# A streaming attention kernel: ScalarE's pairs in one branch loop, four VectorE steps merged or moved

## The chip, the cores and the metric

The kernel runs on one core of one Trainium2 chip. The metric is the device time of that core in microseconds (us); lower is better. Engines are named as in the profile: PE is TensorE's matmuls, PEld its weight loads, DVE is VectorE, ACT is ScalarE, POOL is GpSimd, SP is the engine that issues most DMAs. The suffix q (ACTq, SPq) means the engine's sequencer.

## The reference, cut to what matters

One token (512 values) attends to a cache of 32 heads x 16384 positions x 128, and a small gated MLP of the same token is mixed in:

```python
# shapes: x (1,1,512); k_cache, v_cache (1,32,16384,128) bf16; wq (512,4096); wo (4096,512)
g = sigmoid((x * gate_w).sum(-1, keepdims=True))
q = (x @ wq) split in 32 heads
p = softmax(q k^T / sqrt(128)); o = p v
a = o @ wo
b = gmlp(x, w_in, w_sp, b_sp, w_out)      # small
return g * a + (1 - g) * b
```

K and V are 134 MB each. Every byte is read once and used for one query, so the kernel is a stream from HBM with arithmetic beside it.

## The kernel before

Heads are taken in 16 pairs. One pair has one K load and one V load of 8.39 MB each; three buffers of that size take turns. Load n may be issued when the user of load n-3 is done. SP issues them:

```python
k_at = [max(2 * i - 1, 0) for i in range(NP)]            # K0 K1 V0 K2 V1 K3 V2 ...
v_at = [min(2 * i + 2, 2 * NP - 1) for i in range(NP)]
...
wait = [user[n - 3]] if n >= 3 else ...                  # exps(i) frees a K buffer, values(i) a V buffer
sp.op(lambda e: e.dma_start(out=buf[n % 3][:, ...], in_=src[:, ...]), wait=wait, ...)
```

So the load of V1 waits for the exps of pair 1, V2 for those of pair 2 and so on; K loads from K3 on wait for PE's values. For each pair DVE multiplies K by q in four quarters and PE and DVE sum them to scores, ACT takes the exponentials (`exps`), PE multiplies by V, and ACT copies the result out of the PSUM bank and zeroes it (`renew`):

```python
def exps(e, i):
    take(e, red_s)                      # the scores of pair i are there
    ...                                 # two activations Exp, 64 rows each
def renew(e):
    drain(e).then_inc(zer_s, 1)         # copy the value bank out
    take(e, zer_s)
    e.copy(out=d_ps, in_=zero[:, :]).then_inc(drn_s, 1)

def act_pairs(e):
    e.wait_ge(*p_zero)
    exps(e, 0)
    exps(e, 1)
    with e.Fori(2, NP) as i:
        renew(e)
        exps(e, i)
    renew(e)
    ...
```

The set-up before the pairs (queries, gate, gMLP) and the tail after them (scale, transpose, product with wo) are straight-line code on all engines. The output projection's weights wo are the last bytes of the stream.

The softmax here doesn't subtract the row's maximum and nothing guards it: scores larger than these inputs give would overflow.

## Time and profile before

The time was 652.02 us (median of 3 runs, 651.7 to 652.5).

| | before |
|---|---|
| span of the profiled run | 650.2 us |
| bytes read | 279.6 MB, 430 GB/s over the span |
| DMA engines | 9 tenths or more in all slices but the last |
| busy PE / DVE / ACT | 65% / 52% / 7% |

From the page of the kernel before: the span, the busy times, the DMA row (busy tenths in 40 slices) and the rate in each slice.

```profile
span 650.2 us, 7753 instructions
...
PE 424.3 (65%) x2474; PEld 47.0 (7%) x1312; DVE 335.8 (52%) x159; ACT 45.8 (7%) x112; POOL 2.2 (0%) x10
...
DMA  9999999999999999999999999999999999999998
GB/s 384 463 419 452 452 395 443 452 443 395 452 452 395 443 452 448 391 452 452 403 435 452 448 391 452 452 431 407 452 452 395 443 452 439 399 435 468 392 428 342
...
```

No engine is busy for even 70% of the span, but the DMA engines always are. The Trainium skill ("DMA: Bandwidth & Descriptors", "Where 436 GB/s comes from") gives a ceiling of 435.2 GB/s. This trace agrees: successive 8.39 MB loads land 19.35 us apart (26 loads between the landings at 76.8 and 579.9 us), which is 433.5 GB/s. The same section also says that for loads from HBM a core's share of about 358 GB/s binds; this core, running alone, is above that.

From the chain of waits that ended last, before (start, duration, what):

```profile
...
617.70 0.33 SPq L643
...
619.02 28.88 DMA bufs<-in_A_wo_dram
...
647.94 0.65 PE ps_all L716 x8
...
648.61 0.41 DVE res L731
```

The span ends with the last pieces of wo, then eight matmuls and one copy. SP issues wo's loads at 617.70, when ACT's last exps have freed their buffer (the link before, cut here).

From the timeline of SP, before: the K and V loads as they are issued (start, duration, what).

```profile
...
65.79 0.33 SPq L638 DMA_DIRECT2D bufs<-in_A_k_cache_dram  x1
90.87 0.33 SPq L638 DMA_DIRECT2D bufs<-in_A_v_cache_dram  x1
...
122.68 0.33 SPq L638 DMA_DIRECT2D bufs<-in_A_v_cache_dram  x1
...
```

The profile also tells when each load landed: the K2 load issued at 65.79 took 30.4 us, so it landed at 96.2. ("Landed" means that the last piece of the load had arrived.) The V1 load was issued at 90.87, when the queue still had 96.2 - 90.87 = 5.3 us of work. I call this number the *queue left* at issue. For the steady pairs it is 11 to 12 us for V loads and 21 to 22 us for K loads.

From the timeline before, around the first exps of ACT; the last bracket is the idle time before the piece:

```profile
...
63.14 0.69 DVE L564 TENSOR_REDUCE s_sb<-ps_all 128x64 f32<-128x512 f32 x1 [3.93 <-DVEq L86]
63.96 1.28 ACT L592 ACT_TABLE_LOAD   x1 [29.56 <-ACTq L86]
...
65.79 0.33 SPq L638 DMA_DIRECT2D bufs<-in_A_k_cache_dram  x1
...
```

The Exp table is loaded between the end of the scores (63.83) and the first exps; K2's load follows at 65.79.

From the timeline before, the set-up steps in question:

```profile
...
1.18 0.27 DVE L278 MEMSET sel<- 32x258 uint32 x1 [1.18 <-PEq L762]
...
2.20 3.04 DVE L301 MEMSET ps_all<- 128x3584 f32 x1 [0.74 <-issue]
...
12.03 0.41 DVE L314 TENSOR_TENSOR xg_row<-x_row,gw_row 1x512 bf16<-1x512 bf16 x1 [5.33 <-DMA wb_row<-in_B_b_sp_dram]
...
14.17 0.16 DVE L327 COPY wbf<-ps_all 128x2 f32<-128x2 f32 x1 [0.94 <-ACT gm_sb L325]
...
17.13 0.55 PE L345 MATMUL ps_all<-bufs,xb 128*128 x1 [3.27 <-DMA bufs<-in_B_w_in_dram]
```

VectorE writes `sel` at 1.18, waits until 12.03 for a small DMA, copies `wbf` at 14.17, and PE then waits until 17.13 for w_in. From the same timeline, the tail:

```profile
...
629.44 0.24 DVE L667 TENSOR_SCALAR rl<-rl,g_sb 128x32 f32<-128x32 f32 x1
...
641.17 0.19 DVE L669 TENSOR_TENSOR o_sb<-ps_all,rl 128x32 bf16<-128x32 f32 x1 [11.49 <-PE ps_all L531]
...
647.94 0.38 PEld L716 LDWEIGHTS ps_all<-bufs,o 128*1 128x1 bf16 x8 [0.40 <-DMA bufs<-in_A_wo_dram]
...
```

The scale step (L667) runs at 629.44, long before the multiply (L669) at 641.17. PE's last eight matmuls wait 0.40 us for wo.

### The profile page before, as it was taken

Reading aid. Unit: us, or ns where it says so; the run is one execution under the profiler, and the core shown is the slowest. Engines: PE = TensorE matmul, PEld = TensorE weight load, DVE = VectorE, ACT = ScalarE, POOL = GpSimd, SP = SyncE. Lnnn points to the kernel's source line nnn. Section 1 sums busy time; section 2 is a strip of 40 time slices with the busy share of each in tenths; the row PEclk is TensorE's granted clock in tenths of the full one; section 3 lists DMA queues with packets and bytes.
Section 4 is the critical chain, followed back from the end, with each engine's and each line's share of the span. In section 5 each row is a group of like instructions: output and inputs, shape, how many; then the busy total and the mean of one; then the engine's idle time right before and its main releaser. Section 6 shows DMA issues by size and latency. Waiting matters only on the chain. (4 is left out here: it accounts for less than half of the span.)

```text
span 650.2 us, 7753 instructions
## 1 busy us (share of the span) xinstructions
PE 424.3 (65%) x2474; PEld 47.0 (7%) x1312; DVE 335.8 (52%) x159; ACT 45.8 (7%) x112; POOL 2.2 (0%) x10
## 2 busy tenths in 40 slices
PE   0646687847477574857757486584748857478678
PEld 0000000000101000010000101000010100001022
DVE  3457839256380835628165370835628174465600
ACT  2210000100001000010100001000000100001011
POOL 1000000000000000000000000000000000000000
PEclk9959798958889796888969679796977969698979
DMA  9999999999999999999999999999999999999998
GB/s 384 463 419 452 452 395 443 452 443 395 452 452 395 443 452 448 391 452 452 403 435 452 448 391 452 452 431 407 452 452 395 443 452 439 399 435 468 392 428 342
DMA packets 6203, 279.60 MB, mean 430 GB/s; under 512 B 695, under 2 KB 826, under 8 KB 1210
## 3 DMA queue, kind: packets, MB, share of 16 engines
q1 hardware_dynamic: 6194, 279.58, 99.6%
q8 instruction: 1, 0.02, 0.0%
q10 hardware_dynamic: 8, 0.00, 0.0%
HBM read 279.58 MB, written 0.00 MB: 430 GB/s over the span
## 5 line engine op out<-in xcount | busy, mean ns | idle before, releaser
L579 DVE TENSOR_TENSOR bufs<-bufs,qb x64 | 281.4, 4418 | 170.8 <-DVEq L86 170.8
L91 PE MATMUL ps_all<-bufs,ident 128*128 x960 | 258.8, 423 | 0.0
L496 PE MATMUL ps_all<-bufs,ident 128*128 x64 | 28.6, 446 | 154.2 <-PEq L86 153.9
L106 PE MATMUL ps_all<-bufs,p_t 128*8 x1024 | 82.5, 396 | 30.1 <-PEq L86 20.1
L564 DVE TENSOR_REDUCE s_sb<-ps_all 128x64 f32<-128x512 f32 x64 | 44.0, 687 | 93.1 <-DVEq L86 93.1
L91 PE MATMUL ps_all<-zero,ident 128*8 128x512 bf16 (+2 forms) x167 | 59.5, 388 | 0.0
L592 ACT ACTIVATE p_t<-s_sb 64x256 f32 (+1 forms) x32 | 13.3, 415 | 433.1 <-ACTq L86 432.7
L496 PEld LDWEIGHTS ps_all<-bufs,ident 128*128 128x128 bf16 x64 | 6.3, 99 | 365.6 <-issue 365.6
L106 PEld LDWEIGHTS ps_all<-bufs,p_t 128*8 x1024 | 19.4, 83 | 163.1 <-issue 161.6
L531 PE MATMUL ps_all<-pick,d_sb 128*128 128x2 f32 x128 | 17.0, 255 | 16.5 <-PEq L86 16.5
L531 PEld LDWEIGHTS ps_all<-pick,d_sb 128*128 128x128 f32 x128 | 15.7, 193 | 34.7 <-issue 34.7
L601 ACT COPY d_sb<-ps_all 128x512 f32<-128x512 f32 x16 | 9.4, 586 | 105.4 <-ACTq L86 105.4
L606 ACT CAST ps_all<-zero 128x512 f32<-128x512 bf16 x15 | 8.8, 589 | 1.7
L666 DVE RECIPROCAL rl<-ps_all 128x32 f32<-128x32 f32 x1 | 0.4, 357 | 12.2 <-PE ps_all L552 12.2
L381 DVE TENSOR_TENSOR bufs<-ps_all,ident 128x896 f32<-128x896 f32 x2 | 2.1, 1086 | 8.6 <-PE ps_all L91 8.6
L669 DVE TENSOR_TENSOR o_sb<-ps_all,rl 128x32 bf16<-128x32 f32 x1 | 0.2, 191 | 11.5 <-PE ps_all L531 11.5
L592 ACT ACTIVATION_READ_ACCUMULATOR p_t<-s_sb (+1 forms) x32 | 5.9, 185 | 0.0
L321 PE MATMUL ps_all<-xgw,const-float32-1.0 1*128 1x3 f32 x2 | 0.6, 360 | 8.0 <-DVE xgw L317 8.0
L91 PE MATMUL ps_all<-bufs,xb 128*128 x12 | 5.0, 552 | 0.0
L106 PE MATMUL ps_all<-bufs,u 128*1 x14 | 2.6, 372 | 3.1 <-ACT ps_all L427 2.4
L345 PE MATMUL ps_all<-bufs,xb 128*128 x4 | 2.3, 574 | 3.3 <-DMA bufs<-in_B_w_in_dram 3.3
L106 PE MATMUL ps_all<-bufs,xb 128*64 x32 | 3.6, 380 | 0.0
(76 smaller groups left out, 40.2 us busy)
## 6 DMA issues: line engine op xcount, KB each, us to landing
bufs<-in_A_k_cache_dram SPq DMA_DIRECT2D x2, 4096.0 KB, 36.2
bufs<-in_A_v_cache_dram SPq DMA_DIRECT2D x1, 5120.0 KB, 34.5
bufs<-in_A_wq_dram SPq DMA_DIRECT2D x1, 4096.0 KB, 12.3
bufs<-in_A_v_cache_dram SPq DMA_DIRECT2D x1, 2048.0 KB, 39.0
bufs<-in_A_wo_dram SPq DMA_DIRECT2D x1, 2048.0 KB, 25.4
bufs<-in_B_w_in_dram SPq DMA_DIRECT2D x1, 1792.0 KB, 15.5
bufs<-in_A_v_cache_dram SPq DMA_DIRECT2D x1, 1024.0 KB, 41.0
bufs<-in_A_wo_dram SPq DMA_DIRECT2D x1, 1024.0 KB, 27.6
```

What stands on the lines that cost most here:

```text
L91: ins = eng.matmul(out, lhsT=lhsT, rhs=rhs, **flags).ins
L106: ins = eng.matmul(bank[0:m, 0:n], lhsT=lhsT, rhs=rhs, **flags).ins
L321: g_ok = pe.op(lambda e: e.matmul(g_ps, lhsT=ones_f[0:1, :], rhs=xgw[:, :], start=True, stop=True), wait=[xgw_ok], mark=True)
L345: if n else matmul_on(nc, e, lambda: e.matmul(args[0], lhsT=args[1], rhs=args[2], **flags), [at, (xa, 0)]))
L381: dve.op(lambda e, h=h, zh=zh: e.tensor_tensor(out=zm[:, 2 * h * ZB:2 * (h + 1) * ZB].rearrange("p (b m k) -> p b m k", b=2, k=FhC), in0=z ...
L496: matmul_on(nc, e, lambda: e.matmul(s3, lhsT=ident[:, :], rhs=k3[:, :, 0:W], start=True, **flags), [(kw, 0)])
L531: ins = e.matmul(o2, lhsT=d_sb[:, r * Dh:(r + 1) * Dh], rhs=pick[:, r * 2:(r + 1) * 2], start=False, stop=False, skip_group_check=True)
L564: return e.tensor_reduce(out=s_sb[:, c * QK:(c + 1) * QK], in_=s_ps[c % 2].rearrange("p (j w) -> p j w", w=W), axis=AX.X, op=ALU.add)
L579: e.tensor_tensor(out=k3, in0=k3, in1=qi, op=ALU.mult).then_inc(mul_s, 1)
L592: e.activation(out=p_t[rows, bass.ds(at, NG * 8)].rearrange("p (t c) -> p t c", c=8)[:, :, 4 * s:4 * s + 4], in_=s_sb[rows, :].rearrange(" ...
L601: return e.copy(out=d_sb[:, :], in_=d_ps)
L606: e.copy(out=d_ps, in_=zero[:, :]).then_inc(drn_s, 1)
```

## The change

The intent: ScalarE's instructions become one loop without peeled copies, its Exp table is loaded early, and VectorE loses three instructions and one wait. Main parts of the diff (line shifts and unchanged context cut):

```diff
-    for t in [L_sb, p_t, zero]:
+    for t in [sel, L_sb, p_t, zero]:
         p_zero = pool.op(lambda e, t=t: e.memset(t[:, :], 0.0), mark=True)
+    sel_ok = (pool.sem, ident_ok[1] + 1)
-    const_ok = dve.op(lambda e: e.memset(sel[:, :], 0.0), mark=True)
 ...
     dve.op(lambda e: e.tensor_tensor(out=xg_row[:, :], in0=x_row[:, :], in1=gw_row[:, :],
-                                     op=ALU.mult), wait=[(ld_x, 16), (ld_g, 48)], mark=True)
+                                     op=ALU.mult), wait=[(ld_g, 48)], mark=True)
 ...
-    dve.op(lambda e: e.tensor_copy(out=wbf[:, :], in_=g_ps[:, 1:3]), wait=[gm_ok], mark=True)
-    g_free = dve.chain(lambda e: e.memset(g_ps, 0.0))
+    wbf_ok = act.op(lambda e: e.copy(out=wbf[:, :], in_=g_ps[:, 1:3]), mark=True)
+    g_free = dve.op(lambda e: e.memset(g_ps, 0.0), wait=[wbf_ok], mark=True)
 ...
     def act_pairs(e):
+        kind = [e.engine]
+        i = counter(e, "ia", 0)
         e.wait_ge(*p_zero)
-        exps(e, 0)
-        exps(e, 1)
-        with e.Fori(2, NP) as i:
+        e.activation(out=var[:, :], in_=eps_t[:, :], func=ACT.Exp)
+        nc.br("act_exps", engines=kind)
+        with nc.body("act_renew", valid_engines=kind):
             renew(e)
-            exps(e, i)
+            nc.br("act_exps", engines=kind)
+        with nc.body("act_exps", valid_engines=kind):
+            exps(e, value(e, i, NP - 1))
+            e.reg_alu(i, i, 1, ALU.add)
+            e.br_lt(i, 2, on_true="act_exps", on_false="act_more")
+        with nc.body("act_more", valid_engines=kind):
+            e.br_lt(i, NP, on_true="act_renew", on_false="act_last")
+        nc.switch_bb("act_last")
         renew(e)
 ...
-    dve.chain(lambda e: e.tensor_scalar(out=rl[:, :], in0=rl[:, :], scalar1=g_sb[:, 0:1],
-                                        scalar2=0.0, op0=ALU.mult, op1=ALU.add))
-    o_ok = dve.chain(lambda e: e.tensor_tensor(out=o_sb[:, :], in0=o_ps[:, 0:H], in1=rl[:, :],
-                                               op=ALU.mult), wait=[used_v[-1]])
+    o_ok = dve.chain(lambda e: e.scalar_tensor_tensor(
+        out=o_sb[:, :], in0=o_ps[:, 0:H], scalar=g_sb[:, 0:1], in1=rl[:, :], op0=ALU.mult,
+        op1=ALU.mult), wait=[used_v[-1]])
```

More of the change, by code (lines that the diff above doesn't have):

```diff
@@ L307, in gated_mix_kernel @@
         out=sel[:, :].rearrange("h (i x) -> h i x", x=P + 1)[:, :, 0:P:4],
-        in_=ident[0:H, 0:H].unsqueeze(1).broadcast_to([H, 4, H])), wait=[const_ok, ident_ok],
+        in_=ident[0:H, 0:H].unsqueeze(1).broadcast_to([H, 4, H])), wait=[sel_ok],
         mark=True)
@@ L324, in gated_mix_kernel @@
            wait=[g_ok], mark=True)
-    gm_ok = act.op(lambda e: e.activation(out=gm_sb[:, :], in_=g_ps[:, 0:1], func=ACT.Sigmoid,
+    act.op(lambda e: e.activation(out=gm_sb[:, :], in_=g_ps[:, 0:1], func=ACT.Sigmoid,
                                           scale=-1.0), mark=True)
-    dve.op(lambda e: e.tensor_copy(out=wbf[:, :], in_=g_ps[:, 1:3]), wait=[gm_ok], mark=True)
-    g_free = dve.chain(lambda e: e.memset(g_ps, 0.0))
+    wbf_ok = act.op(lambda e: e.copy(out=wbf[:, :], in_=g_ps[:, 1:3]), mark=True)
+    g_free = dve.op(lambda e: e.memset(g_ps, 0.0), wait=[wbf_ok], mark=True)
     def pe_gmlp(e):
```

## The prediction

> **What bounds the kernel.** The DMA engines. The page counts 279.60 MB in a span of 650.2 us, 430 GB/s; its DMA row shows 9 in every slice but the last; queue 1 alone fills 99.6% of the span. PE is busy 65%, DVE 52%, ACT 7%. The Trainium skill ("DMA: Bandwidth & Descriptors", "Where 436 GB/s comes from") gives a port ceiling of 435.2 GB/s; this trace agrees. The chain that ended last is one wait for the last pieces of wo (28.88 us, to 647.89), eight matmuls (0.65 us) and DVE's output copy (0.41 us); of ACT only the exps that let the wo loads be issued at 617.7.
>
> **Is the queue ever short?** From the issue times (the timeline of SP) and the bytes issued before each, at the mean rate, I estimate how long the queue still had work when each load was issued: 4.5 us at the smallest (V, issued at 90.9 us), then about 11 us for V and 21 us for K loads. The issues wait for ACT's exps (424 us in SP's waits), so ACT's timing sets them, but a delay must pass those slacks to cost anything.
>
> **What the change does.**
> 1. ACT's pairs become one loop with a counter; the order of waits and work stays. It adds about one jump and one compare-and-branch per pair: the Trainium skill ("Advanced Engine Details and Errata", "Control Flow Timing") gives 51 and 108 ns, so 0.15 us a pair, 2.5 us summed (estimate; the trace doesn't count branches). ACT waits 432.7 us for the scores, so most hides; the rest delays an issue by 0.2 us against 4.5 or more.
> 2. The Exp table load (1.28 us at 63.96, after the first scores' end and before the first exps) moves into ACT's idle 30 us before, with a dummy 128x1 activation (about 0.17 us, as the sigmoid at L323). The K load issued at 65.79 comes 1.3 us earlier; the queue had 10 us of work: gain 0.
> 3. sel's memset (DVE, 0.27 us) goes to Pool (estimate 0.53 us, as for zero), ready near 2.4; ACT's copy starts at 3.38, after its table load. DVE then waits for wb_row until 12.03: gain 0.
> 4. wbf's copy goes from DVE (0.16 us) to ACT, before PE's gMLP matmuls, which wait for w_in until 17.12: gain 0.
> 5. In the tail a tensor_scalar (0.24 us) is merged into the multiply (0.19 us). It ran at 629.4, long before the last values (641.17): saves nothing. The merged instruction may take 0.03 to 0.1 us longer (estimate; the 128x1 one at L410 took 0.22). It is on the chain to wo's matmuls, where PE idled 0.40 us for the last DMA: absorbed.
>
> On the critical path: about 0 us. Bytes, order and first DMA issue are unchanged.
>
> **Prediction.** 652.0 us, 650.7 to 653.3 in 8 of 10. Faster by over 2%: 0.01; within 2%: 0.97; slower by over 2%: 0.02.
>
> **What would show it.** 279.6 MB at about 430 GB/s; the same chain with a wo wait near 29 us; no table load near 64 us, and the third K load issued near 64.5; ACT busy up 0.3 us; DVE down 0.6 us, three instructions fewer; PE's idle before the last eight matmuls still above 0.
>
> **What would make it wrong.** Branches that cost ACT microseconds[...] and push V issues past 4.5 to 11 us; a table load inside the loop; a merged step over 0.4 us slower; another DMA rate in that run.

## The result

The changed kernel took 651.9 us (median of 6 runs, 651.44 to 653.03) against 651.68 us (6 runs, 651.54 to 652.5). The ratio is 1.0004 with a 95% interval of 0.9991 to 1.0017: the same time. A ratio here is the mean time of one kernel's fast runs over that of the other's fast runs of the same rounds, so it is not quite the ratio of the quoted medians.

From the page of the changed kernel, the same lines:

```profile
span 650.0 us, 7779 instructions
...
PE 424.7 (65%) x2474; PEld 46.1 (7%) x1312; DVE 335.2 (52%) x156; ACT 46.1 (7%) x114; POOL 2.6 (0%) x11
...
DMA  9999989999998999999999989999998999999898
GB/s 386 473 407 452 452 387 452 452 432 407 452 452 387 452 452 448 391 452 452 391 448 452 452 387 452 452 407 432 452 452 387 452 452 423 415 419 484 387 431 345
...
```

Bytes, rate and span agree. VectorE has three instructions fewer and 0.6 us less work; ScalarE has 0.3 us more. The DMA row has some eights where it had nines, but the K and V loads land on the same beat, 19.3 to 19.4 us apart.

The chain of waits that ended last, after:

```profile
...
617.66 0.33 SPq L652
...
618.99 28.71 DMA bufs<-in_A_wo_dram
...
647.74 0.65 PE ps_all L724 x8
...
648.41 0.41 DVE res L739
```

It has the same links, with 28.71 us for 28.88. The timeline around the first exps, after:

```profile
...
63.03 0.69 DVE L564 TENSOR_REDUCE s_sb<-ps_all 128x64 f32<-128x512 f32 x1 [3.93 <-DVEq L86]
...
64.03 0.42 ACT L592 ACTIVATE p_t<-s_sb 64x256 f32 x1 [28.23 <-ACTq L86]
...
64.57 0.33 SPq L647 DMA_DIRECT2D bufs<-in_A_k_cache_dram  x1
...
```

The table load has left this place and K2's load goes out at 64.57 instead of 65.79. The 1.22 us so gained end in a longer queue: K2 is issued with about 12 us of queue left instead of 11.0, and it lands one beat of the stream after V0, as before. The gap from the end of the scores (63.03 + 0.69 = 63.72) to the exps is 0.31 us, where the table load began after 0.13: with a counter in a register, ScalarE works out addresses after the wait. For pair 1 the same gap grew from 0.12 to 0.30 us.

The set-up steps, after:

```profile
...
1.77 0.52 POOL L276 MEMSET sel<- 32x516 bf16 x1
1.90 3.04 DVE L301 MEMSET ps_all<- 128x3584 f32 x1 [1.90 <-PEq L770]
...
12.09 0.41 DVE L314 TENSOR_TENSOR xg_row<-x_row,gw_row 1x512 bf16<-1x512 bf16 x1 [5.24 <-DMA wb_row<-in_B_b_sp_dram]
...
14.08 0.17 ACT L327 COPY wbf<-ps_all 128x2 f32<-128x2 f32 x1
...
16.89 0.55 PE L345 MATMUL ps_all<-bufs,xb 128*128 x1 [2.96 <-DMA bufs<-in_B_w_in_dram]
```

`sel` is now written by POOL (0.52 us), `wbf` copied by ACT, and both are done long before what follows them. VectorE's first big memset starts at 1.90 instead of 2.20, and VectorE still waits for the small DMA until 12.09.

The tail, after:

```profile
...
640.94 0.25 DVE L676 SCALAR_TENSOR_TENSOR o_sb<-ps_all,g_sb,rl 128x32 bf16<-128x32 f32 x1 [11.72 <-PE ps_all L531]
...
647.74 0.40 PEld L724 LDWEIGHTS ps_all<-bufs,o 128*1 128x1 bf16 x8 [0.38 <-DMA bufs<-in_A_wo_dram]
...
```

The merged step takes 0.25 us where the multiply took 0.19, and PE still waits 0.38 us for wo.

### The profile page after: what moved, and what is told of

It reads as the page before. It is cut to its first block, busy times and chain, and to the rows that moved or that the text cites. A ratio compares the mean times of both kernels' runs of the same rounds, so it can differ in the third digit from the quotient of the medians.

```text
span 650.0 us, 7779 instructions
## 1 busy us (share of the span) xinstructions
PE 424.7 (65%) x2474; PEld 46.1 (7%) x1312; DVE 335.2 (52%) x156; ACT 46.1 (7%) x114; POOL 2.6 (0%) x11
## 5 line engine op out<-in xcount | busy, mean ns | idle before, releaser
L106 PE MATMUL ps_all<-bufs,p_t 128*8 x1024 | 80.7, 389 | 31.0 <-PEq L86 20.9
L592 ACT ACTIVATE p_t<-s_sb 64x256 f32 x32 | 13.3, 414 | 462.6 <-ACTq L86 462.2
L592 ACT ACTIVATION_READ_ACCUMULATOR p_t<-s_sb x32 | 5.9, 184 | 0.0
L301 DVE MEMSET ps_all<- 128x3584 f32 x1 | 3.0, 3045 | 1.9 <-PEq L770 1.9
```

Of the source, the lines that this page charges most:

```text
L106: ins = eng.matmul(bank[0:m, 0:n], lhsT=lhsT, rhs=rhs, **flags).ins
L301: dve.op(lambda e: e.memset(ps_all[:, 0:7 * 512], 0.0), mark=True)
L592: e.activation(out=p_t[rows, bass.ds(at, NG * 8)].rearrange("p (t c) -> p t c", c=8)[:, :, 4 * s:4 * s + 4], in_=s_sb[rows, :].rearrange(" ...
```

## The experiments

Theory A: the DMA stream sets the time, and what the change touches lies in slack. Its rivals: B, the parts of the change do act but cancel; C, ScalarE's step is on the path of every pair; D, the queue is deep enough for any delay; later E, F and G, as they came up. "Late" below means landing more than 19.35 us after the load ahead.

### Experiment 1: the branch loop alone

The edit is the `act_pairs` part of the diff, put on the kernel before.

> The kernel before with ScalarE's pairs as the branch loop and the early Exp table load, nothing else changed. Theory A (the DMA stream sets the time, and what the change touches lies in slack): ratio 1.000 to within 0.0015, the K load issued at 64.5 instead of 65.8 us, the V load of pair 1 about 0.13 us later than before, neither visible in the time. Rival B (the parts do have effects, which cancel in the whole change: the early table load gains 1.3 us, the branches or the tail lose as much): a gain of 1 us or more here (ratio 0.998 or lower) or a loss of 1 us or more, with the opposite sign in the run with the set-up steps alone.

It measured 651.73 us against 652.04, ratio 0.9996 (0.9982 to 1.0010). In its profiled run K2's load went out at 65.46 us, not at the expected 64.5, and V1's at 92.19 with 4.1 us of queue left, over a microsecond later than the 90.87 of before; V1 still landed in step, 19.35 us after K2.

The two profiles differ by more than the loop explains. Over the ten profiled runs without an added ScalarE delay in pairs 0 and 1, V1's issue lay between 90.7 and 92.6, and it goes with the clock that the throttle granted to PE. PE is busy all the time from 71 to 78 us, on the scores of pair 1; the granted clock in this stretch was 0.80 before (issue at 90.87), 0.73 in experiment 2 (91.67), 0.70 here (92.19), and 0.66 and 0.64 in experiments 10 and 5 (92.47 and 92.59). Experiments 4 and 9, at 0.86, don't keep the order (91.09 and 91.34). No run sets the clock on purpose, so this is a correlation.

### Experiment 2: the four set-up steps alone

The edit is the rest of the diff, with ScalarE's old loop.

> The kernel before with only the four VectorE steps merged or moved (sel to Pool, wbf to ScalarE, the dropped wait, the merged tail multiply), ScalarE's loop as before. Theory A: ratio 1.000 to within 0.0015; VectorE busy 0.6 us less; PE's idle before the last eight matmuls stays near 0.4 us. Rival B: opposite in sign to the run with the loop alone, and 1 us or more.

It measured 651.87 us, ratio 0.9998 (0.9984 to 1.0012); DVE was busy 335.2 us (335.8 before), and PE's idle before the last eight matmuls was 0.38 us. Neither half shows an effect, within intervals of about 1 us to either side. Rival B, which needs two effects of 1 us or more with opposite signs, falls.

### Experiment 3: a delay of four copies before the exps of every pair

This and the next runs dose the delay, to see whether slack is the reason. On the changed kernel:

```diff
     def exps(e, i):
         take(e, red_s)
+        for _ in range(4):
+            e.copy(out=idle[:, :].rearrange("p (r x) -> p r x", r=4),
+                   in_=zero[:, :].unsqueeze(1).broadcast_to([P, 4, 512])).then_inc(idle_s, 1)
+            take(e, idle_s)
```

> The changed kernel with four scratch copies (about 1.9 us each, 7.6 to 8 us in all) on ScalarE before the exps of every pair. Theory A: it passes the smallest slack only, the 4.4 us of the V load of pair 1, where the delay of pair 0 also holds up the scores of pair 1; the steady slack of about 10 to 11 us holds. So the stream stops once, near 95 us, and the time rises by 3 to 8 us (estimate 6.6), not by 16 x 8 = 128. Rival C (ScalarE's step is on the critical path of every pair, hidden only because its changes were small): plus 100 us or more. Rival D (the queue is deep enough everywhere): plus 0.

It measured 669.77 us, ratio 1.0271 (1.0255 to 1.0287), so plus 17.7 us. C (plus 100) and D (plus 0) fall, but A's plus 3 to 8 is missed as well. From its timeline of SP, the loads K2 and V1:

```profile
...
73.65 0.33 SPq L652 DMA_DIRECT2D bufs<-in_A_k_cache_dram  x1
104.85 0.33 SPq L652 DMA_DIRECT2D bufs<-in_A_v_cache_dram  x1
...
```

K2 was issued with 3.2 us left and landed 0.9 us late. V1, issued 7.7 us after the queue had run out, landed 29.5 us after K2, 10.2 us late. These 11.1 us are the stop that A expected, but larger than its 3 to 8 us. Later loads, in pairs where A still saw slack, add 5.7 us, and a longer tail about 2 us.

### Experiment 4: the same delay for pairs 2 to 15 only

The same four copies, on the variant of experiment 2, only where `i` is not a constant (pairs 2 to 15):

```diff
+        for _ in range(0 if isinstance(i, int) else 4):
```

> The same four scratch copies (about 7.9 us) on ScalarE, but before the exps of pairs 2 to 15 alone (on the variant with the set-up steps and the old loop, where pairs 0 and 1 stand apart). Theory A: 7.9 us is below the steady slack of 10 to 11 us: ratio 1.000 within 0.002, although ScalarE works 110 us more. Rival C: plus 100 us.

It measured 659.76 us, ratio 1.0120 (1.0102 to 1.0139), plus 7.7 us. So A as first put is wrong about the size of the slack. The timeline of ACT in this run, pair 2:

```profile
...
123.21 7.93 ACT L591 COPY idle<-zero 128x2048 bf16<-128x2048 bf16 x4 [24.04 <-ACTq L86]
131.44 0.42 ACT L597 ACTIVATE p_t<-s_sb 64x256 f32 x1 [0.31 <-ACTq L86]
...
```

The four copies, with their waits, hold the exps back by 8.2 us (123.21 to 131.44). From the timeline of SP in this run, the loads K8 and V7:

```profile
...
290.54 0.33 SPq L643 DMA_DIRECT2D bufs<-in_A_k_cache_dram  x1
326.85 0.33 SPq L643 DMA_DIRECT2D bufs<-in_A_v_cache_dram  x1
...
```

K8's time to landing was 39.5 us, so it landed at 330.1, and V7 was issued with 3.2 us of queue left. V7's time to landing was 24.3 us: it landed at 351.1, 21.0 us after K8, 1.7 us late, though the queue had not run out when it was issued. Five V loads (V2, V5, V7, V9, V11) went out with 2.9 to 3.7 us of queue left and landed 0.6 to 1.7 us late, 6.0 us in all; the V loads in between (to V13) went out with 3.9 to 5.7 us left and landed within 0.15 us of the beat. One load doesn't fit: V14 had 3.05 us left and landed in step (the text below the dose table returns to it). The rest of this run's span (8.9 us more than before) is a tail that no longer waits for wo: its chain ends in PE's matmuls.

From here on theory A': as A, but a load must be issued about 4 us before the load ahead of it lands. That leaves the steady V loads of the changed kernel some 7 us of room (11 less 4) and V1 about 1 us (5.0 less 4). This is a rule of thumb from the loads above.

### Experiment 5: half the delay for pairs 2 to 15

`range(0 if isinstance(i, int) else 2)` in place of 4.

> Half the delay of the run before: two scratch copies (about 4.2 us with their waits) before the exps of pairs 2 to 15. Theory A' (the stream sets the time, but a load must be issued about 4 us before the landing of the load ahead of it, not 0 to 2 us as theory A had it; read from the late landings of the four-copy run, where loads issued with 2.9 to 3.7 us of queue left landed 0.5 to 1.8 us late and those with 3.9 or more did not): V loads then go out with 7 to 8 us of queue left, so ratio 1.000 within 0.002 and every landing 19.3 to 19.4 us after the one before. Rival C (every microsecond of delay costs in proportion): half of the 7.7 us, about plus 4.

It measured 651.69 us, ratio 0.9996 (0.9979 to 1.0012). The V loads from V2 on went out with 6.9 to 8.1 us left, and all landed 19.3 to 19.4 us after the load ahead. Some 4.2 us of delay in each of 14 pairs cost nothing, although 8.2 us cost 7.7: this is a threshold, not a price per microsecond, and C falls in its mild form too. (In the profiled run V1, which this edit doesn't touch, was issued with 3.5 us left and landed 0.9 us late; the granted clock before it was the lowest of the ten runs, see experiment 1. The room at V1 is small enough for an ordinary run to use it up.)

### Experiment 6: the same copies where ScalarE is idle

On the variant of experiment 2, the four copies stand at the end of `renew`:

```diff
         e.copy(out=d_ps, in_=zero[:, :]).then_inc(drn_s, 1)
+        for _ in range(4):
+            e.copy(out=idle[:, :].rearrange("p (r x) -> p r x", r=4), ...)...
```

> The same four scratch copies per pair, about 7.9 us of ScalarE work, but put after the zeroing of the value bank, where ScalarE then waits some 24 us for the scores, so that the exps are not delayed. Theory A': ratio 1.000 within 0.002; V loads issued with 11 to 12 us of queue left. Rival E (the copies' own memory traffic slows the stream, not the late issues): plus 7 to 9 us as in the four-copy run.

It measured 651.93 us, ratio 1.0001 (0.9984 to 1.0017). From its timeline of ACT:

```profile
...
98.71 7.93 ACT L609 COPY idle<-zero 128x2048 bf16<-128x2048 bf16 x4
122.05 0.42 ACT L593 ACTIVATE p_t<-s_sb 64x256 f32 x1 [15.40 <-ACTq L86]
...
```

The copies are done 15 us before the exps need ScalarE. ScalarE was busy 158.9 us, more than the 152.1 of experiment 4, and the time is that of before. So the copies' own traffic is not what slowed experiment 4 (rival E falls); the late issues are.

### Experiment 7: two copies before the exps of every pair

As experiment 3 with `range(2)`.

> Two scratch copies (about 4.2 us) before the exps of all pairs, on the changed kernel. Theory A': only the V load of pair 1 falls below 4 us of queue left (5.0 us in the changed kernel, minus 4.2, minus about 1 for pair 0's delay that holds up pair 1's scores: about 0); it lands 2.5 to 4.5 us late and the time rises by that. Theory A as first put (slack 4.4 us, no lead): 0 to plus 1. Rival C: plus 8.

It measured 655.49 us, ratio 1.0052 (1.0035 to 1.0068), plus 3.8 us: inside the 2.5 to 4.5 of A', outside the other two. From its timeline of SP, the loads K2 and V1:

```profile
...
69.38 0.33 SPq L652 DMA_DIRECT2D bufs<-in_A_k_cache_dram  x1
96.75 0.33 SPq L652 DMA_DIRECT2D bufs<-in_A_v_cache_dram  x1
...
```

K2 landed at 69.38 + 26.8 = 96.2. V1 was issued about 0.6 us after that and landed 21.8 us after its issue, 3.0 us late. V3 was 0.4 us late although it had 7.9 us left, which A' doesn't explain; all other loads to V13 landed within 0.15 us of the beat. One late load makes most of the difference here.

### Experiment 8: half of one V load left out

```diff
+        if kind == "v" and i == 8:
+            cuts = (0, KP // 2)
```

Pair 8 then uses old data for half of its V (the comparison with the reference still passed, so it is no evidence that this result is right). Its output is wrong, which doesn't matter for the time.

> The changed kernel with half of one V load left out (pair 8 of 16; 4.19 MB of 279.6; the result is wrong on purpose). Theory A': the time falls by the bytes over the stream's rate, 4.19 MB at 433 GB/s = 9.7 us, to about 642.2 us, because compute follows the landings. A rival in which PE or VectorE work sets the time: no fall, since they do the same work.

It measured 643.17 us, ratio 0.9865 (0.9849 to 0.9882), minus 8.5 us, with all arithmetic still done. From its timeline of SP, the loads V8 (the halved one), K10 and V9:

```profile
...
354.76 0.33 SPq L649 DMA_DIRECT2D bufs<-in_A_v_cache_dram  x1
364.07 0.33 SPq L649 DMA_DIRECT2D bufs<-in_A_k_cache_dram  x1
394.59 0.33 SPq L649 DMA_DIRECT2D bufs<-in_A_v_cache_dram  x1
```

V8's landing came 9.7 us after the load ahead, as expected. But the stream was now ahead of compute: K10 landed at 364.07 + 32.0 = 396.1, so V9 was issued with 1.5 us left and landed 0.8 us late, and two later loads, V11 and K13, were late by 0.2 and 0.4 us. Together that is about the missing 1.2 us. The time follows the bytes, and V9's late issue takes a part back; V11 and K13 had 11.3 and 21.6 us left, so why they were late is open.

### Experiment 9: a delay in the tail

Three scratch memsets on VectorE between `o_sb` and the transpose:

```diff
+    for _ in range(3):
+        o_ok = dve.chain(lambda e: e.memset(idle[:, :], 0.0))
```

> The changed kernel with three scratch memsets (about 0.95 us each, near 2.9 us in all) on VectorE after the merged multiply that makes o_sb, ahead of wo's matmuls. Theory A': the tail has 0.38 us of room (PE's idle before the last eight matmuls), so the end moves by about 2.5 us (652 to 654.5, ratio near 1.004) and PE's wait for the last wo piece vanishes. Rival F (the tail has microseconds of room, wo's landing hides it): plus 0 to 0.5.

It measured 656.07 us, ratio 1.0065 (1.0051 to 1.0079), plus 4.4 us. From its timeline, the tail:

```profile
...
641.26 0.25 DVE L677 SCALAR_TENSOR_TENSOR o_sb<-ps_all,g_sb,rl 128x32 bf16<-128x32 f32 x1 [11.76 <-PE ps_all L532]
...
641.79 0.91 DVE L681 MEMSET idle<- 128x1024 uint32 x1 [0.28 <-DVE o_sb L677]
...
645.14 0.29 PE L684 MATMUL ps_all<-ident,o_sb 128*32 128x128 bf16 x1 [3.46 <-DVE idle L681]
...
```

The first matmul after `o_sb` starts 3.88 us after it (641.26 to 645.14) where it was 0.35 us in the changed kernel (640.94 to 641.29): 3.5 us of delay, as each memset also has 0.28 us of waiting that the expectation left out. PE's wait for wo is gone. The expected 2.5 us was too low for that reason; PE's first 16 matmuls for wo also took 0.6 us (median) in place of 0.4 after the longer pause, whose part in the end time no run separates. Rival F falls: beyond about 0.4 us the tail has no room.

### Experiment 10: a delay in VectorE's set-up

Five scratch memsets before VectorE's first big memset, on the changed kernel:

```diff
+    for _ in range(5):
+        dve.chain(lambda e: e.memset(idle[:, :], 0.0))
     dve.op(lambda e: e.memset(ps_all[:, 0:7 * 512], 0.0), mark=True)
```

> The changed kernel with five scratch memsets (about 0.95 us each, near 4.8 us in all) on VectorE before its first big memset, eight times what the change took from VectorE in set-up (0.43 us). Theory A': VectorE then waits less for wb_row (which lands near 12.1 us), everything after that at the same times: ratio 1.000 within 0.0015. Rival G (VectorE's set-up steps are on the way to the first scores or to the V load at 36 us): plus 3 to 5 us.

It measured 652.07 us, ratio 1.0002 (0.9988 to 1.0016). (The expectation's "eight times" is eleven by its own numbers, 4.8 over 0.43.) From its timeline of DVE:

```profile
...
7.76 3.04 DVE L304 MEMSET ps_all<- 128x3584 f32 x1 [0.74 <-issue]
...
12.04 0.41 DVE L317 TENSOR_TENSOR xg_row<-x_row,gw_row 1x512 bf16<-1x512 bf16 x1
...
```

The big memset starts at 7.76 instead of 1.90, and the multiply that waits for the small DMA starts at 12.04, as ever. VectorE had over 5 us to spare at this place, so the 0.27 us of `sel` was never worth anything there. Rival G falls. (In this profile V1 went out at 92.47 with 3.6 us left and landed 0.7 us late; experiment 5's profile, without this delay, has V1 at 92.59, so the delay need not be the reason. The profiled runs of experiments 5 and 10, with V1 late, took 652.46 and 652.18 us; those of before, changed and experiments 1, 2 and 6, with V1 in step, took 651.44 to 651.75. A part of the spread between runs of one kernel may be this.)

### The dose, in one table

Queue left is the landing of the load ahead (its issue plus its time to landing) minus the issue of this one; the beat is 19.35 us. The values are worked out from the trace's own times, rounded to 0.1 us.

| run, load | issued at | queue left | landed after the load ahead | late |
|---|---|---|---|---|
| before, V1 | 90.87 | 5.3 us | 19.3 us | 0 |
| changed, V1 | 91.00 | 5.0 | 19.4 | 0 |
| experiment 1, V1 | 92.19 | 4.1 | 19.4 | 0 |
| experiment 4, V6 | 286.53 | 4.9 | 19.3 | 0 |
| experiment 4, V14 | 602.83 | 3.0 | 19.4 | 0 |
| experiment 4, V7 | 326.85 | 3.2 | 21.0 | 1.7 |
| experiment 4, V2 | 131.98 | 2.9 | 19.9 | 0.6 |
| experiment 8, V9 | 394.59 | 1.5 | 20.1 | 0.8 |
| experiment 7, V1 | 96.75 | -0.6 | 22.4 | 3.0 |
| experiment 3, V1 | 104.85 | -7.7 | 29.5 | 10.2 |

With an empty queue a load needs 21.8 us from issue to landing (experiments 3 and 7), 2.45 us more than the beat. The packets in the trace show where these go: a load is 128 packets of 64 KB, 16 at a time, of 2.42 us each (8 in a row make the beat). In experiment 7 the first packets of V1 started 1.0 to 1.7 us after its issue, and took 2.8 to 3.3 us.

With 2.9 to 3.7 us left, loads were late by 0.2 to 1.7 us, but for two (V14 in experiments 3 and 4) that landed in step; with 3.9 or more, by 0.4 us at most.

Why is 3 us not always enough, when the empty-queue cost is 2.45, and why is it sometimes? The landing is the last of 16 increments of the load's semaphore. The packed trace keeps the other 15 too, though `prof` doesn't print them; I take each for one of the 16 DMA engines. They lie within 0.7 us before and 0.3 us in the changed kernel. In experiment 4 the late loads draw them apart: by 0.6 us for the load ahead of V2, 1.9 us ahead of V7, 2.9 us ahead of V13. So V7 had 3.2 us left by the last increment, but 1.4 us by the first: most engines were done with K8 more than 1 us before it landed.

By the mean of the 16 increments the loads fall in order: those with 1.2 to 1.9 us left were 0.6 to 1.3 us late, V14 of both runs among them; with 2.4 to 3.4 us, 0 to 0.5; with more than 3.4 us, 0.2 at most, but for two (0.4) that had 7.7 and 21.4 us left and stay unexplained. The lead of "some 4 us" by the last increment thus holds for engines that end close together.

The DMA row of the page doesn't show these losses. In experiment 4 it has a 9 in every slice but the last, as before: the time is lost in packets that took up to 3.8 us in place of 2.42, and these count as busy.

## Why the prediction was right

**The time.** 652.0 us was predicted and 651.9 measured; "about 0 on the critical path" was right, and experiments 1, 2 and 10 show it for the parts, not only for the sum.

**What bounds the kernel.** Right: leaving out 4.19 MB took 8.5 us off with all the arithmetic kept (experiment 8), and 113 us of extra ScalarE work in idle time cost nothing (experiment 6: busy 158.9 us against 45.8 in experiment 2).

**Is the queue ever short.** The mechanism was right and its size was off. "4.5 us at the smallest, then about 11 us for V and 21 us for K" describes the queue at issue well (5.3, 11 to 12, 21 to 22 from the landings). But the prediction read these numbers as the room: "a delay must pass those slacks to cost anything". The runs show that some 4 us of it are needed by the issue itself, so the room is about 1 us at V1 and 7 us in the steady pairs. Delays of 0.2 us fit into both, so the forecast held; a change that delayed pair 1 by 2 us would probably have been misjudged (V1 with 3.5 us left was 0.7 to 0.9 us late in experiments 5 and 10). That the error didn't matter was partly luck: in these two runs V1's room was used up with no delay of its own, and there the loop's 0.2 us could have been paid in full. It would still be below the noise.

**1, the loop.** Right in effect. Its cost was put at "51 and 108 ns" from the Trainium skill ("Advanced Engine Details and Errata", "Control Flow Timing"), with the remark that the trace doesn't count branches. The trace does have records of them, not counted as busy: ScalarE's compare-and-branch records last 34 to 50 ns (31 of them in the loop, against 14 before). The larger part of the loop's cost is elsewhere: the 0.18 us of register work after the wait in pairs 0 and 1, which the prediction did not name.

**2, the table load.** Right: it moved to 34.3 us, its dummy activation took 0.20 us (0.17 estimated), and K2 went out at 64.57 (64.5 predicted).

**3 and 4, the set-up steps.** Right: `sel` was ready at 2.29, and PE's gMLP matmuls still waited for w_in, to 16.89.

**5, the tail.** Right: the merged step took 0.06 us longer (0.03 to 0.1 estimated), absorbed in PE's wait, which shrank from 0.40 to 0.38 us. Experiment 9 shows how near this was to mattering.

**No faster version.** The stream already lands its loads at 433.5 GB/s without a gap. The 279.6 MB at that rate are 645.0 us; start, tail and what lies outside the span are the other 7 us. None of the runs points to a version that beats both kernels.

## What to carry to other kernels

When the DMA row is full, ask of a change first two things: does it alter the bytes, and does it delay an issue beyond the queue left minus the lead that an issue needs (some 4 us here)? A row of nines alone doesn't say that the stream keeps its beat: look at the landings. Read the queue left from issue times and landings, load by load, because the tightest load (here one of the start-up, with 5 us) is not the typical one. A flat result for a small change doesn't prove slack; a delay given in two doses, and the same work placed where it delays nothing, does.

## What the Trainium skill lacked or had wrong

- "DMA: Bandwidth & Descriptors", "Latency and other measured facts", gives about 600 ns to the first byte for hardware-issued DMAs and speaks of a fixed cost of about 2 us; it doesn't say how far ahead of the end of the queue a large load must be issued. Here an 8.39 MB load on an empty queue cost 2.45 us more than in a full one, and with 2.9 to 3.7 us of queue left loads were still up to 1.7 us late; from 3.9 us on they were late by 0.4 us at most.
- "ScalarE: Activation LUTs", "What ACT_TABLE_LOAD costs", gives about 1283 ns plus a drain of about 1380 ns. The load's record is 1283 ns here too, but from the end of the scores to the first exps it took 1.43 us with the load (63.83 to 65.26, before) and 0.31 us without it (63.72 to 64.03, after); no second part of that size shows. (ScalarE had been idle for 29.56 us before this load, so the case doesn't test a load right behind work.)
- "Advanced Engine Details and Errata", "Control Flow Timing", gives about 108 ns for a compare-and-branch; ScalarE's records of it last 34 to 50 ns in the changed kernel (the time around the record is not in that).
